# Pooling sums of an attention kernel: values summed in thirds on POOL, the keys' first level made over all partitions, with copies by ACT

## The chip, the cores and the metric
The kernel runs on one core of one Trainium2 chip. The metric is the time on the device in microseconds (us) of one execution, as the median of several runs.

## The reference
There are four batches of eight heads; each head has 576 tokens of 64 numbers, in float32. An attention with two branches feeds two mixture-of-experts layers with 8 experts each (width 512, hidden width 1024).

```python
q_d = q.reshape(B, H, Sd, 4, D).mean(axis=3)     # k_d, v_d alike: Sd = 144
out_up = np.repeat(sm_attn(q_d, k_d, v_d), 4, axis=2)
mask = np.abs(pos[:, None] - pos[None, :]) < 4   # the local branch: 7 keys for each query
out_local = softmax(where(mask, scale * q @ k.T, -1e9)) @ v
x = (out_up + out_local)  ->  [2304, 512]
x = moe(x, w1, w2, gates)                        # top 1 of 8: relu(x @ w1[e]) @ w2[e], weighted
x = moe2(x, w1, w2, gate)
```

The change concerns only how q, k and v are summed over groups of four tokens for the pooled branch (the division by four is folded into later scales).

## The kernel before
**Layout.** Two heads are stacked on the 128 partitions, so that partitions 0 to 63 hold one head of a pair and 64 to 127 the other; NP = 4 pairs make the eight heads. `kd` and `qt` hold keys and queries of a batch transposed (three buffers each, for batches b % 3). `vraw` holds the values of one batch in the order of the pooled branch, as 128 x (3 chunks of keys, 4 tokens of a group, 4 pairs, 65); it has one buffer, so the load of the next batch's values waits until the last sum of this one has read it.

**The sums of four.** `sums_q` and `sums_k` sum four neighbouring tokens. On DVE a single `tensor_reduce` does it (line 465). On POOL it takes two additions: a first level into a temporary `tm` (line 467), which halves four to two, and a second level (line 468). The keys' sums go into `kpd`, which is block diagonal: the upper 64 partitions are summed into one block and the lower 64 into the other, so `sums_k` runs its whole work once for each half of the partitions. `sums_v` (line 470) adds within `vraw` in place over 128 x 1560 elements (line 471), and then writes the second level of each half of the partitions, 64 x 780 elements, into the block-diagonal `vpd` (line 474).

**Who does what.** Batch 0 stands in a prologue (the string `PRO`): the keys' sums and `sums_v` are on DVE (steps F0, F2 and V0), two pairs at a time. The queries of pairs 0 and 1 need no sums there (the product with them is made four times instead); those of pairs 2 and 3 are summed on DVE. In batch 1 the keys and values are summed by POOL and the queries by DVE; in batches 2 and 3 POOL sums all three.

**The loop behind it.** A software pipeline takes one tile of up to 116 tokens of the local branch in each step: scores on PE, `smax` on DVE (lines 614 and 618, both read PSUM), exponentials on ACT (L623), `norm` on DVE (lines 627 to 630, from SBUF to SBUF), transposes on PE (L635) that ACT evacuates, and the products with the values (L663). The pooled branch of the next batch is mixed in: scores (L503, L512), `smax` (L521, L524), exponentials (L531), transposes (L538), the product with `vpd` (L552, L558), and its `norm` (lines 574 to 584; L584 subtracts one SBUF tensor from another). After each group of four or five tiles `route` finds the expert and the place of every token (lines 254 to 360), in many short DVE instructions; `place` (lines 307 to 338) and `spread` (lines 340 to 353, `am` and `oc` from DVE, `bm` from ACT) feed PE's `list` products (L357). One PSUM bank (`misc`) serves in turn the gate's logits (L377) and the counts `pos` (read by L309 and L311).

**Order.** The scheduler of the language plans the order on each engine by a timeline of its own, from the program's order; the engines then run their queues in order. The experts follow the attention, with PE as the engine that is nearly always busy.

Of the kernel before, what the change touches and what calls it, by code (L numbers as in the profile page):

```python
# [9 lines left out]
F32 = mybir.dt.float32  # L10
# [4 lines left out]
ALU = mybir.AluOpType  # L15
# [5 lines left out]
B, H, S, D = 4, 8, 576, 64  # L21
NP = H // 2
SD = S // 4
# [157 lines left out]
def moe_pair_kernel(  # L181
# [17 lines left out]
    nc = tc.nc  # L199
# [189 lines left out]
    def attention(actx, early, early_x, front):  # L389
# [3 lines left out]
        sb2 = actx.enter_context(tc.tile_pool(name="a_sb2", bufs=2, side="right"))  # L393
# [5 lines left out]
        kd, qt = kq  # L399
        vd = [side[i].tile([128, NG, NP, D], F32, name=f"vd{i}") for i in range(2)]  # L400
        kpd = [side[i].tile([128, 2, NP, SD], F32, name=f"kpd{i}") for i in range(2)]
        vraw = sbe.tile([128, 3, 4, NP, 65], F32, name="vraw")
        vpd = [side[i].tile([128, 3, 2, NP, 65], F32, name=f"vpd{i}") for i in range(2)]
# [38 lines left out]
        def sums_k(b, c, n, eng=None):  # L442
            eng = eng or nc.vector
            a = slice(c, c + n)
            tm = tmp() if eng is nc.gpsimd else None
            for s in range(2):
                o = slice(64 * s, 64 * s + 64)
                src = kd[b % 3][o, a, 3:3 + S].rearrange("p a (t r) -> p a t r", r=4)
                pool4(eng, kpd[b % 2][o, s, a], src, tm[o, 0:n] if tm else None)

        def sums_q(b, c, n, eng=None):
            eng = eng or nc.vector
# [7 lines left out]
        def tmp():  # L460
            return sbe.tile([128, 2, SD, 2], F32, tag="tm", name="tm", bufs=2)

        def pool4(eng, dst, src, tm):
            if tm is None:
                eng.tensor_reduce(dst, src, axis=AX.X, op=ALU.add)
                return
            eng.tensor_tensor(tm, src[:, :, :, 0:2], src[:, :, :, 2:4], op=ALU.add)
            eng.tensor_tensor(dst, tm[:, :, :, 0], tm[:, :, :, 1], op=ALU.add)

        def sums_v(b, eng=nc.gpsimd):  # L470
            eng.tensor_tensor(vraw[:, :, 0:2], vraw[:, :, 0:2], vraw[:, :, 2:4], op=ALU.add)
            for s in range(2):
                o = 64 * s
                eng.tensor_tensor(
                    vpd[b % 2][o:o + 64, :, s], vraw[o:o + 64, :, 0], vraw[o:o + 64, :, 1], op=ALU.add
                )

        def sums(b, eng_q=None):
            for c in (0, 2):
                sums_k(b, c, 2, nc.gpsimd)  # L480
                sums_q(b, c, 2, eng_q or nc.gpsimd)
# [264 lines left out]
        for i in range(3):  # L746
            t = sb3.tile([128, 3, 128], F32, tag="p", name="p")
# [19 lines left out]
        def first(c):  # L767
            sums_k(0, c, 2, nc.gpsimd if c and KPOOL else None)
            if QPE < c + 2:
                sums_q(0, c, 2)  # L770
# [5 lines left out]
        def sums1(c):  # L776
            sums_k(1, c, 2, None if S1[c] == "d" else nc.gpsimd)
            sums_q(1, c, 2, None if S1[c + 1] == "d" else nc.gpsimd)

        pro = {  # L780
            "F0": lambda: first(0),
            "F2": lambda: first(2),
            "V0": lambda: sums_v(0, nc.vector),
            "Ls": lambda: (loc[0].scores(), loc[0].smax()),
            "Le": loc[0].exps,
# [7 lines left out]
            "lqk": lambda: load_qk(1),  # L793
            "lw1": lambda: (load_vw(1), load_qk(2)),
            "V1": lambda: sums_v(1),
            "A0": lambda: sums1(0),
            "A2": lambda: sums1(2),
# [8 lines left out]
        for s in range(-1, NL + 3):  # L806
# [6 lines left out]
            if 0 <= s:  # L813
                b, r = s // NTP + 1, s % NTP
                if b + 1 < B:
                    if r == 0:
                        load_vr(b + 1)
                    if r == (1 if s > 4 else 2):
                        sums_v(b + 1)
                    if r == 0 and b == 2:  # L820
                        load_qk(3)
                if 2 <= b < B and r == 0:
                    sums(b)
# [86 lines left out]
            if 6 <= s < 12:  # L910
                o = 384 * (s - 6)
# [704 lines left out]
```

## Time and profile before
| | |
|---|---|
| time, median of 3 runs | 759.45 us (757.87 to 759.95) |
| the profiled execution | 755.45 us |
| its span | 753.7 us |
| mean granted TensorE clock, share of full speed | 0.967 |
| busy share of the span: PE, DVE, ACT, POOL | 93%, 61%, 45%, 23% |

PE is TensorE's matmuls, DVE is VectorE, ACT is ScalarE, POOL is GpSimd. In a row of the timeline stand the start and the duration in us, the engine, the line, the operation, the tile written and the tiles read with their shapes, how many instructions are merged in the row (x2), and in brackets the engine's idle time before it and what ended it. In a row of a tile's view stand the least, median and greatest duration in ns and the first and last start in us. In a row of the windows stand the window, its length, and for each engine its busy time in it; then the granted TensorE clock, the share of time of the DMA engines and GB/s.

### The profile page before, as it was taken

To read this page: it belongs to the slowest core of one execution; us is meant where nothing else is said; L and a number is where in the kernel's file an instruction comes from. 1 tells how busy PE (TensorE), PEld (TensorE's weight loads), DVE (VectorE), ACT (ScalarE), POOL (GpSimd) and SP (SyncE) were. 2 spreads that over 40 slices of the span, in tenths; PEclk is the share of its full clock that TensorE was granted. 3 is DMA by queue.
4 is the path that set the end of the run, shared out by engine and by line. 5 is a ranking of instruction groups with operands and counts; after the bars stand their busy time and mean duration, and the time that the engine had idled before them with its cause. 6 is when DMAs were issued, how large, how long until landed. Compare 5 with 4: busy or idle time off the path is not lost. (4 is left out here: it accounts for less than half of the span.)

```text
span 753.7 us, 15825 instructions
## 1 busy us (share of the span) xinstructions
PE 700.1 (93%) x6048; PEld 642.4 (85%) x6048; DVE 460.0 (61%) x1169; ACT 342.4 (45%) x630; POOL 173.5 (23%) x202
## 2 busy tenths in 40 slices
PE   6788699995989999999999999989999999999993
PEld 4557477874979999999999999978999999999992
DVE  8787968786847656565757777535434444455520
ACT  2244366574444435345454463235425353554530
POOL 5774800001031203031211120152013030311111
PEclk9899989996999999999999999989999999999997
DMA  9935635135167535364555452256443544655500
GB/s 359 407 117 205 213 116 186 49 119 169 34 217 220 166 120 171 128 201 134 164 193 167 165 179 97 93 187 214 137 137 130 158 159 155 196 173 192 161 21 16
DMA packets 52990, 120.99 MB, mean 161 GB/s; under 512 B 4800, under 2 KB 26176, under 8 KB 51884
## 3 DMA queue, kind: packets, MB, share of 16 engines
q1 hardware_dynamic: 45772, 99.19, 39.6%
q0 software_dynamic: 7136, 20.72, 8.0%
q8 instruction: 50, 0.82, 0.4%
q14 instruction: 32, 0.26, 0.1%
HBM read 101.01 MB, written 20.71 MB: 162 GB/s over the span
## 5 line engine op out<-in xcount | busy, mean ns | idle before, releaser
L1123 DVE TENSOR_TENSOR wl<-raw,wh 128x1024 fp32r<-128x1024 f32 x128 | 156.2, 1224 | 111.2 <-ACT wh L1115 111.1
L1115 ACT CAST wh<-raw 128x1024 fp32r<-128x1024 f32 x128 | 133.1, 1048 | 199.1 <-PE py L1277 114.3
L1277 PE MATMUL ph<-xl,wh 128*128 128x256 f32 (+8 forms) x576 | 178.1, 311 | 0.2 <-DVE xl L1201 0.2
L1276 PE MATMUL ph<-xh,wh 128*128 128x256 f32 (+8 forms) x576 | 175.0, 312 | 2.6 <-DVE xl L1201 1.9
L1278 PE MATMUL ph<-xh,wl 128*128 128x256 f32 (+8 forms) x576 | 177.2, 309 | 0.0
L1276 PE MATMUL py<-h,wh 128*128 128x256 f32 (+8 forms) x448 | 138.5, 316 | 0.0
L1277 PE MATMUL py<-h,wh 128*128 128x256 f32 (+8 forms) x448 | 137.8, 311 | 0.0
L1278 PE MATMUL py<-h,wl 128*128 128x256 f32 (+8 forms) x448 | 137.3, 309 | 0.0
L1276 PEld LDWEIGHTS ph<-xh,wh 128*128 128x128 f32 x576 | 110.6, 195 | 4.8 <-DVE xl L1201 2.0
L1277 PEld LDWEIGHTS ph<-xl,wh 128*128 128x128 f32 x576 | 111.5, 194 | 1.1 <-DVE xl L1201 0.5
L1278 PEld LDWEIGHTS ph<-xh,wl 128*128 128x128 f32 x576 | 111.5, 194 | 0.6
L1403 DVE SCALAR_TENSOR_TENSOR h<-ph,h 128x256 fp32r<-128x256 f32 (+8 forms) x144 | 66.3, 471 | 40.9 <-ACT h L1402 40.4
L1402 ACT ACTIVATE h<-ph 128x256 fp32r<-128x256 f32 (+8 forms) x144 | 60.8, 423 | 55.9 <-PE ph L1278 54.7
L1277 PEld LDWEIGHTS py<-h,wh 128*128 128x128 f32 x448 | 84.2, 188 | 0.6
L1278 PEld LDWEIGHTS py<-h,wl 128*128 128x128 f32 x448 | 84.1, 188 | 0.6
L1276 PEld LDWEIGHTS py<-h,wh 128*128 128x128 f32 x448 | 83.5, 188 | 0.8
L1144 POOL DMA_INDIRECT xr<-x,ri x49 | 49.9, 1019 | 102.3 <-PE t L1194 79.4
L1204 POOL DMA_INDIRECT out<-yr,ri x25 | 25.8, 1031 | 128.9 <-ACT yr L1222 84.6
L1204 POOL DMA_INDIRECT x<-yr,ri x24 | 24.4, 1016 | 126.5 <-ACT yr L1222 118.0
L1476 DVE COPY yT<-py 128x256 f32<-128x256 f32 (+8 forms) x28 | 13.7, 489 | 39.9 <-PE py L1278 39.9
L1201 DVE TENSOR_TENSOR xl<-t,xh 128x512 fp32r<-128x512 f32 (+5 forms) x49 | 30.1, 620 | 12.2 <-ACT xh L1198 12.0
L1194 PE MATMUL t<-ident,xr 128*128 128x128 f32 (+5 forms) x196 | 29.6, 272 | 8.5 <-DMA xr<-x,ri 8.5
(193 smaller groups left out, 1037.3 us busy)
## 6 DMA issues: line engine op xcount, KB each, us to landing
raw<-w_a SPq DMA_DIRECT2D x64, 512.0 KB
raw<-w_b SPq DMA_DIRECT2D x64, 512.0 KB
vraw<-vr SPq DMA_DIRECT2D x4, 1560.0 KB
vd<-vw SPq DMA_DIRECT2D x4, 1280.0 KB
kd<-kT SPq DMA_DIRECT2D x8, 586.0 KB
qt<-qT SPq DMA_DIRECT2D x8, 586.0 KB
x<-zx SPq DMA_DIRECT2D x6, 768.0 KB
x<-x SPq DMA_DIRECT2D x36, 116.0 KB
```

What stands on the lines that cost most here:

```text
L1115: i = nc.scalar.copy(hi, raw)
L1123: i = nc.vector.tensor_tensor(lo, raw, hi.bitcast(F32), op=ALU.subtract)
L1144: g = nc.gpsimd.indirect_dma_start(xr[0:mm], None, src, bass.IndirectOffsetOnAxis(ap=ri[0:mm, k, 0:1], axis=0))
L1194: nc.tensor.transpose(pt[:, d, 0:mm], xr[0:mm, 128 * d:128 * d + 128], ident[0:mm, 0:mm])
L1201: nc.vector.tensor_tensor(xl[:, :, o], pt[:, :, 0:mm], xh[:, :, o].bitcast(F32), op=ALU.subtract)
L1204: i = nc.gpsimd.indirect_dma_start(M.dst[:, :], bass.IndirectOffsetOnAxis(ap=ri[0:mm, k, 1:2], axis=0), yr[0:mm], None, bounds_check=NT - ...
L1276: nc.tensor.matmul(ps, lhsT=ah, rhs=bh, start=first, stop=False)
L1277: nc.tensor.matmul(ps, lhsT=ah, rhs=bl, start=False, stop=False)
L1278: nc.tensor.matmul(ps, lhsT=al, rhs=bh, start=False, stop=last)
L1402: nc.scalar.activation(a[:, 0:n], ph[:, 0:n], func=AF.Relu)
L1403: nc.vector.scalar_tensor_tensor(b_[:, 0:n], ph[:, 0:n], 0.0, a[:, 0:n].bitcast(F32), op0=ALU.max, op1=ALU.subtract)
L1476: nc.vector.tensor_copy(yT[:, dc, 0:n], py[:, 0:n])
```

## The change
The keys' sums: on DVE (batch 0) one `tensor_reduce` over all 128 partitions writes a temporary `ks` with one buffer, and two copies by ACT put its halves in their blocks of `kpd`. On POOL (batches 1 to 3) the first addition is made once over all partitions, the second still for each half. The values' sums, on POOL and in batch 0 on DVE, go in three chunks: for each of the three, an addition of 128 x 520 and two of 64 x 260.

```diff
         def sums_k(b, c, n, eng=None):
             eng = eng or nc.vector
             a = slice(c, c + n)
-            tm = tmp() if eng is nc.gpsimd else None
+            src = kd[b % 3][:, a, 3:3 + S].rearrange("p a (t r) -> p a t r", r=4)
+            if eng is nc.vector:
+                tm = sb2.tile([128, 2, SD], F32, tag="ks", name="ks", bufs=1)[:, 0:n]
+                pool4(eng, tm, src, None)
+            else:
+                tm = tmp()[:, 0:n]
+                eng.tensor_tensor(tm, src[:, :, :, 0:2], src[:, :, :, 2:4], op=ALU.add)
             for s in range(2):
                 o = slice(64 * s, 64 * s + 64)
-                src = kd[b % 3][o, a, 3:3 + S].rearrange("p a (t r) -> p a t r", r=4)
-                pool4(eng, kpd[b % 2][o, s, a], src, tm[o, 0:n] if tm else None)
+                if eng is nc.vector:
+                    nc.scalar.copy(kpd[b % 2][o, s, a], tm[o])
+                else:
+                    eng.tensor_tensor(kpd[b % 2][o, s, a], tm[o, :, :, 0], tm[o, :, :, 1], op=ALU.add)
...
         def sums_v(b, eng=nc.gpsimd):
-            eng.tensor_tensor(vraw[:, :, 0:2], vraw[:, :, 0:2], vraw[:, :, 2:4], op=ALU.add)
-            for s in range(2):
-                o = 64 * s
-                eng.tensor_tensor(
-                    vpd[b % 2][o:o + 64, :, s], vraw[o:o + 64, :, 0], vraw[o:o + 64, :, 1], op=ALU.add
-                )
+            for k in range(3):
+                eng.tensor_tensor(vraw[:, k, 0:2], vraw[:, k, 0:2], vraw[:, k, 2:4], op=ALU.add)
+                for s in range(2):
+                    o = slice(64 * s, 64 * s + 64)
+                    eng.tensor_tensor(vpd[b % 2][o, k, s], vraw[o, k, 0], vraw[o, k, 1], op=ALU.add)
```

## Rows read from the trace of the kernel before
**Rows 1.** Windows: busy time of each engine in stretches of the span.
```profile
8.00:29.00 21.00, 13.08 (x117) 10.42 (x116) 20.65 (x37) 5.83 (x13) 10.08 (x11) 0.84 1.02 413
...
84.00:97.00 13.00, 6.37 (x104) 4.65 (x105) 12.96 (x33) 4.96 (x14) 7.17 (x3) 0.85 0.42 157
97.00:160.00 63.00, 61.43 (x1059) 49.75 (x1058) 49.19 (x180) 38.64 (x95) 0.00 (x0) 0.98 0.33 108
...
280.00:400.00 120.00, 120.00 (x872) 115.67 (x871) 76.33 (x210) 58.21 (x97) 26.30 (x35) 1.00 0.51 165
```
**Rows 2.** Timeline of DVE in the first batch, 4 to 22 us.
```profile
4.62 2.73 DVE L465 TENSOR_REDUCE kpd<-kd 64x288 f32<-64x1152 f32 x2 [1.78 <-DMA kd<-kT]
7.97 2.71 DVE L465 TENSOR_REDUCE kpd<-kd 64x288 f32<-64x1152 f32 x2 [0.62 <-DMA kd<-kT]
10.72 1.35 DVE L465 TENSOR_REDUCE qd<-qt 128x288 f32<-128x1152 f32 x1
...
14.04 1.77 DVE L471 TENSOR_TENSOR vraw<-vraw 128x1560 f32<-128x1560 f32 x1
...
17.66 2.83 DVE L474 TENSOR_TENSOR vpd<-vraw 64x780 f32<-64x780 f32 x2
20.52 0.82 DVE L524 TENSOR_TENSOR pd<-s,pmx 128x288 f32<-128x288 f32 x2
```
**Rows 3.** Timeline of PE, where it had stood idle ahead of 60 us.
```profile
21.08 2.41 PE L538 MATMUL t<-ident,pd 128*128 128x128 f32 x9 [5.77 <-issue]
...
47.22 0.55 PE L538 MATMUL t<-ident,pd 128*128 128x128 f32 x3 [2.49 <-ACT pd L531]
```
**Rows 4.** Timeline of ACT: its first work after the table load.
```profile
13.20 0.81 ACT L531 ACTIVATE pd<-pd 128x288 f32<-128x288 f32 x2 [11.18 <-DVE pd L524]
```
**Rows 5.** Tile vraw: the sums of the values on both engines.
```profile
L474 POOL TENSOR_TENSOR vpd<-vraw x6: 1817/1838/2283, 47.1 to 90.9; 64x780 f32<-64x780 f32 x6
...
L471 POOL TENSOR_TENSOR vraw<-vraw x3: 3484/3501/3511, 42.2 to 85.5; 128x1560 f32<-128x1560 f32 x3
L474 DVE TENSOR_TENSOR vpd<-vraw x2: 990/1400/1810, 17.7 to 18.7; 64x780 f32<-64x780 f32 x2
```
**Rows 6.** Tile tm: the first level of keys and queries on POOL.
```profile
L467 POOL TENSOR_TENSOR tm<-kd x12: 1136/1144/1764, 16.7 to 78.8; 64x576 f32<-64x576 f32 x12
L467 POOL TENSOR_TENSOR tm<-qt x4: 1197/1206/1206, 34.9 to 80.0; 128x576 f32<-128x576 f32 x4
```
**Rows 7.** Timeline of DVE, 27 to 46 us: additions from SBUF to SBUF.
```profile
27.73 0.69 DVE L630 TENSOR_TENSOR p<-p,sm 128x512 f32<-128x512 f32 x1
...
29.23 0.43 DVE L584 TENSOR_TENSOR odl<-od,odh 128x256 fp32r<-128x256 f32 x1 [0.47 <-ACT odh L583]
...
40.17 1.53 DVE L630 TENSOR_TENSOR p<-p,sm 128x512 f32<-128x512 f32 x1
41.63 4.20 DVE L584 TENSOR_TENSOR od2l<-od,od2h 128x128 fp32r<-128x128 f32 x1
```
**Rows 8.** Timeline of POOL in the same stretch.
```profile
41.11 1.11 POOL L468 TENSOR_TENSOR kpd<-tm 64x288 f32<-64x288 f32 x1
42.19 3.48 POOL L471 TENSOR_TENSOR vraw<-vraw 128x1560 f32<-128x1560 f32 x1
```
**Rows 9.** Timeline of DVE, 86 to 93 us: three short instructions of route's place.
```profile
86.09 2.88 DVE L327 SCALAR_TENSOR_TENSOR den<-den,ez 128x5 f32<-128x5 f32 x1
...
89.12 1.79 DVE L310 TENSOR_TENSOR pe<-pe,oh 128x40 f32<-128x40 f32 x1
...
91.10 1.69 DVE L336 COPY v<-gh 128x5 f32<-128x5 f32 x1
```
**Rows 10.** Timeline of PE in the same stretch, after its two longest idle times.
```profile
91.13 0.42 PE L377 MATMUL lT<-xT,wg 128*32 128x128 f32 x8 [2.74 <-DVE gh L334]
...
95.85 0.73 PE L357 MATMUL list<-bm,am 128*128 128x432 f32 x1 [3.56 <-ACT bm L348]
```

## The prediction, made before the changed kernel was built or run
> **What bounds the kernel now.** I read the busy time by stretches first, to see which engine sets the pace where. In the experts' part PE is busy all the time (120.00 of 120 us in the stretch shown), and from 97 to 160 us nearly so, 61.43 of 63 [rows 1]. Whatever is won ahead of 97 us should therefore reach the end one for one, since behind that point the same PE work waits for its turn. Ahead of it there are two stretches in which DVE and not PE is full: 8 to 29 us (DVE 20.65 of 21, PE 13.08) and 84 to 97 us (DVE 12.96 of 13, PE 6.37) [rows 1]. The change works in both, and in a place between.
>
> Then the timelines of DVE, and of POOL and PE beside it. Three places matter.
>
> First batch. DVE sums the keys in two pairs of reduces, at 4.62 and 7.97 us; each pair had waited for its keys to land. Behind the second it has work without a break, the queries' sum, V0 (its additions at 14.04 and 17.66), and the subtraction at 20.52 [rows 2]. PE's transposes start at 21.08 after 5.77 us of idleness, just behind that subtraction, which frees a PSUM buffer [rows 3].
>
> At 42 us. A DVE subtraction of 128x128 begins at 41.63 and lasts 4.20 us, where one twice that size took 0.43 earlier [rows 7]. In the same stretch POOL ends an addition at 42.22 and has its first level of values, 3.48 us long, from 42.19 to 45.67 [rows 8]. DVE is let go at 45.83, as POOL ends. So an operation of DVE with two inputs in SBUF is held while POOL adds. PE lacked work for 2.49 us, up to 47.22 [rows 3].
>
> At 86 us. The same happens three times in a row: L327, L310 and L336, on 5 to 40 elements a partition, take 2.88, 1.79 and 1.69 us [rows 9], where 128x256 took 0.43 [rows 7]; at least 5.1 us of the 6.36 are waiting. POOL's first level begins at 85.5 and lasts 3.5, the two second-level additions 1.84 each, the last from 90.9 [rows 5]; each of the three is let go as one of POOL's ends. PE idles 2.74 us up to 91.13 (the logits wait for the bank that the place step reads) and 3.56 us up to 95.85 (the first list product) [rows 10].
>
> **The change part by part.**
>
> *Keys of batch 0.* Four reduces of half the partitions become two over all. One of 128x288 costs 1.35 us, a pair of halves 2.71 to 2.73 [rows 2], so 1.36 go twice. The first saving is not on the path: DVE would wait longer for the second keys, which landed at 7.97. The second is, since DVE runs on without a break: **-1.35 us**. Were nothing limited by landings, both would count, -2.7; if DVE then waits for the second queries, which come behind the keys, the gain is 0. The four copies by ACT, of 64x288, are about 0.4 us each, from ACT's 0.81 for two of 128x288; ACT stood idle for 11.18 us up to 13.20 [rows 4], so they hide there. Without that cover they would cost PE 0.8 us a pair.
>
> *Values of batch 0 on DVE.* The first level of 1.77 us becomes three of 128x520, 0.69 each by the 128x512 of [rows 7]; two second-level additions of 0.99 unheld [rows 5] become six of 64x260, 0.43 each by the 128x256 of [rows 7]. That is 2.07 + 2.58 against 1.77 + 1.98: **+0.90 us**, on the path by the same argument. Lower bound 0, if back-to-back starts hide the fixed parts. The upper bound has to take in the holds: one of the two second-level additions was held already (1.81 against 0.99 [rows 5]).
>
> *Keys on POOL.* Six additions of 64x576 go, at 1.14 us, and the six left grow to 1.20, the price of 128 partitions [rows 6]: 6.5 us of POOL over three batches. Count **0** for it: nothing found above waits for the keys' sums, only for POOL's hold to end.
>
> *Values on POOL.* 3.50 us become three of about 1.2 (a 128x576 took 1.20 [rows 6]), and two of 1.84 [rows 5] six of about 0.63. Over a batch this is 7.4 us where 7.2 were, so POOL gains nothing. What changes is how long one hold lasts. At 42 us, the held subtraction would be free after the first third, at 43.4 and not at 45.7, 2.3 us sooner. The later thirds will catch other DVE work, so I take **-2.0 us**; bounds 0 (POOL starts its next piece without a gap, as at 42.19) and -2.49, all that PE idled there.
>
> The Trainium skill, "SBUF — State Buffer", section "Who interferes with whom", says that a Vector instruction with two SBUF inputs and a GpSimd instruction that reads SBUF exclude each other for a whole instruction, and that whoever issues first wins. By it, the subtraction issued at 41.63 should have gone ahead of the addition issued at 42.19; the row shows it behind. By the rule the thirds give the full 2.3 us, by that row 0 where pieces follow without a gap.
>
> Around 86 us the same POOL work has to pass, and DVE is full, so the length of a hold matters less than how much DVE does between holds. Before, three instructions were caught in 7.2 us. With nine pieces DVE gets six more chances to slip one short instruction through, each with the unheld work around it, some 0.25 us (estimate from the unheld 0.43 of a far larger one): **-1.5 us**. Bounds: 0, if every chance is lost to the next piece, and -4.7, if L327 is let go 2.3 us sooner and the other two 1.2 each with nothing caught later. In batch 2 I count 0 either way, since I found no idle time of PE behind its sums.
>
> **Sum.** -1.35 + 0.90 - 2.0 - 1.5 = -3.95, say -4.0 us. The profiled execution took 755.45 us, so 751.45; the median of the runs, 759.45, stands 4.0 above it, and the forecast on that scale is 755.5. A measurement of this kernel can tell some 0.3%, 2.3 us, from no change.
>
> **The rivals.**
>
> *Thirds, but no handover (chance 0.22).* POOL's second piece starts as the first ends, and DVE stays locked out over all nine. For it: at 42.19 POOL went on although DVE had waited since 41.63 [rows 7, 8]. Against it: L327 ended at 88.97, with the first level, and L310 at 90.91, between the two second-level additions [rows 9], so DVE did get in twice; a second level also has to wait for the first. Then only the first batch counts, -0.45, and the place at 86 us perhaps -0.5: 758.5, no change that can be measured.
>
> *The gaps close altogether (0.17).* The clock granted to PE was 0.85 of full in 84 to 97 us, between its two levels of 1.2 and 2.4 GHz, after idle times of 2.74 and 3.56 us; it was 0.98 in the stretch behind [rows 1, 10]. If DVE's hold no longer makes these gaps, the products behind them also run at full clock: 2.49 at 42 us, 4.7 at 86, some 1.5 of clock (0.13 of 13 us is 1.7) and 0.45 in the first batch, -9: 750.5. Against it: DVE is full in that stretch even with 5.1 us of holds taken off (12.96 of 13, so 7.9 are work) and POOL's 7.2 us have to pass in it.
>
> *More pieces catch more DVE work (0.16), the slower side.* Each of the 27 pieces on POOL, and each of V0's nine on DVE, can hold the other engine. Before, POOL's values held DVE for 3.9 us at 42 and at least 5.1 at 86. DVE meets pieces all the time where it is full; at 86 us each of POOL's three caught one [rows 9]. If 16 or more of the 27 pieces catch an instruction on the path, at the mean of 7.4/9 = 0.8 us, they hold 13 us, against 9 now, and V0's pieces, held by POOL's 1.14 to 1.76 us additions that start at 16.7 [rows 6], add up to 1.8 more on two of them. From 14 pieces on it loses; 17 pieces give +4.6, with -0.45 and the 0.5 to 1 of a hold in V0 some +5: 764. Against it: POOL's values take 7.4 us instead of 7.2, so the time in which a hold can fall is the same, and an instruction that is caught waits for a third of what it waited for.
>
> **How the numbers follow.** My forecast, a gain of 2.3 to 6.5 us, has 0.45 and its own range is 753.0 to 757.2. The rivals have 0.22 (758.5), 0.17 (750.5) and 0.16 (764). Faster is the forecast with the second rival, less a little for forecasts that fall short of 2.3: 0.60. Same is the first rival and that little, 0.25. Slower is the third, 0.15. The range of 8 in 10 goes from the second rival's 750.5 to half way to the third's price: 750.0 to 761.0. The scheduler plans anew and may order other work differently; that is why the range doesn't stop at the first rival.
>
> **What would show it.** Right: two reduces of 128x288 from the keys, and four ACT copies ended ahead of 13 us; PE's first transposes ahead of 21.08; no DVE instruction at the first POOL values held for more than 1.3 us, and PE's 2.49 us idle time gone; in the last batch, DVE holds of 0.6 to 1.2 us each, more of them, and the list product ahead of 95.85 by more than the earlier gains. Wrong: DVE held across several pieces; or V0's nine additions spread past 21 us; or PE's gaps at 90 to 96 us as long as before; or a wait of equal length elsewhere, for the experts' first weights above all, that takes back what was won.

## The result and the profile after

| | before | after |
|---|---|---|
| median of the runs (4 each) | 758.89 us | 745.51 us (744.15 to 747.58) |
| ratio, with its 95% interval | | 0.9833 [0.9806, 0.9859] |
| the profiled execution | 755.45 us | 745.73 us |
| its span | 753.7 us | 744.0 us |

The kernel became 13.4 us faster by the medians and 9.7 by the two profiled executions; that of before lies 3.4 us under its median, that of after 0.2 above. The forecast was 755.5 us with a range from 750.0 to 761.0: the direction was right, and the time lies below the range.

The first view is that of the windows of the changed kernel: window, length, busy time of PE, PEld, DVE, ACT and POOL, then the granted clock.

```profile
8.00:29.00 21.00, 13.25 (x113) 10.19 (x112) 20.18 (x38) 6.55 (x14) 6.88 (x9) 0.82 1.02 414
29.00:38.00 9.00, 8.04 (x42) 4.71 (x43) 3.77 (x13) 1.29 (x3) 1.86 (x3) 0.67 0.93 382
...
84.00:97.00 13.00, 11.08 (x147) 8.42 (x145) 12.35 (x35) 9.77 (x28) 6.57 (x6) 1.00 0.70 249
97.00:160.00 63.00, 59.85 (x1083) 49.03 (x1082) 50.06 (x189) 38.89 (x96) 2.72 (x5) 1.00 0.39 139
```

The stretch from 84 to 97 us has changed most. PE works 11.08 us of 13, where it worked 6.37, at a granted clock of 1.00 where it was 0.85 [rows 1]. DVE is as full as before, but with the work of a later tile; PE is nearly full from 97 us on, as it was. The first batch has gained nothing: DVE is still full in it (20.18 us of 21), and behind it, from 29 to 38 us, the granted clock is 0.67, between PE's two levels of 1.2 and 2.4 GHz (more on that below).

To see where the time comes from, I followed the same matmuls on PE through both traces. The order of the instructions differs somewhat between 12 and 15 us and from 54 us on (below), but the same 1108 matmuls stand ahead of the first product with `od2h` of batch 1's last tile.

| what PE begins | before | after | difference | forecast of the step |
|---|---|---|---|---|
| first product with `odh` | 34.03 | 36.97 | +2.9 | -0.45 |
| batch 1's first transposes of `pd` | 47.22 | 47.51 | +0.3 (step -2.65) | -2.0 |
| first product with `od2h`, batch 1's last tile | 107.19 | 96.19 | -11.0 (step -11.3) | -1.5 |
| first transposes of the experts | 177.02 | 167.25 | -9.8 | 0 |
| end of the span | 753.7 | 744.0 | -9.7 | 0 |

Behind the experts' first transposes nothing more is won or lost, as predicted; 1.2 us are lost between the last tile and them. The gain lies between 47 and 107 us.

**First batch.** The timeline of DVE and that of PE in the changed kernel:

```profile
4.49 1.35 DVE L473 TENSOR_REDUCE ks<-kd 128x288 f32<-128x1152 f32 x1 [1.65 <-DMA kd<-kT]
7.78 1.35 DVE L473 TENSOR_REDUCE ks<-kd 128x288 f32<-128x1152 f32 x1 [1.94 <-DMA kd<-kT]
...
14.18 1.91 DVE L480 TENSOR_TENSOR vraw<-vraw 128x520 f32<-128x520 f32 x3
...
16.97 1.75 DVE L483 TENSOR_TENSOR vpd<-vraw 64x260 f32<-64x260 f32 x2
...
19.48 3.36 DVE L483 TENSOR_TENSOR vpd<-vraw 64x260 f32<-64x260 f32 x4
```
```profile
21.64 0.80 PE L559 MATMUL v<-vpd,pts 128*128 128x130 f32 x2 [2.31 <-DVE vpd L483]
...
29.34 0.73 PE L247 MATMUL list<-zb,za 128*128 128x432 f32 x1 [3.04 <-DVE za L246]
```

The keys cost what was predicted, 1.35 us for a pair instead of 2.71 and 2.73 [rows 2]. The six second-level additions of V0 take 5.11 us instead of the 2.58 worked out: POOL's sums for batch 1 hold them. PE waits for their pieces (2.31 us), and then 3.04 us for `za`, the zeros that open the list product.

The 2.9 us by which the first product with `odh` is later have two parts. The product with `za` begins at 29.34 us instead of 27.64, and that is the work of V0's pieces: in the five traces with V0 in nine pieces it begins at 28.68 to 30.46, in all others at 26.74 to 28.19. The other 1.2 us came with the granted clock behind it, and this can't be put down to the change. The windows of the kernel before, and of an experiment below ("whole values behind the places") whose program and order on PE are those of the kernel before up to there:

```profile
29.00:38.00 9.00, 8.24 (x106) 5.55 (x110) 3.94 (x10) 3.01 (x7) 6.05 (x7) 1.00 0.93 383
```
```profile
29.00:38.00 9.00, 8.38 (x43) 4.48 (x42) 2.65 (x7) 1.17 (x4) 3.40 (x4) 0.64 0.93 383
```

With the same program the first product with `odh` came, in these two, at 34.03 us at a clock of 1.00 and at 36.68 at 0.64. So two traces of the same program can differ by some 2.7 us from here on. The trace of the kernel before is an early one; that may be a part of the 3.4 us by which it lies under its median.

**At 42 us.** One view with DVE and POOL together:

```profile
43.06 1.53 POOL L475 TENSOR_TENSOR tm<-qt 128x576 f32<-128x576 f32 x1
43.46 1.29 DVE L591 TENSOR_TENSOR od2l<-od,od2h 128x128 fp32r<-128x128 f32 x1
44.56 3.83 POOL L480 TENSOR_TENSOR vraw<-vraw 128x520 f32<-128x520 f32 x3
```

The subtraction takes 1.29 us instead of 4.20 [rows 7], and PE's idle time of 2.49 us is gone [rows 3]. But the thirds are not what let it in: it came while POOL added queries (L475) and was done at 44.75, about as the first third began. Before, one half of the keys' second level stood ahead of the values [rows 8].

**At 86 us.** The short instructions of `place`, in DVE's timeline, and POOL's values in its own:

```profile
81.50 0.57 DVE L310 TENSOR_TENSOR pe<-pe,oh 128x40 f32<-128x40 f32 x1
...
83.09 0.15 DVE L327 SCALAR_TENSOR_TENSOR den<-den,ez 128x5 f32<-128x5 f32 x1
...
85.15 0.16 DVE L336 COPY v<-gh 128x5 f32<-128x5 f32 x1
```
```profile
76.71 5.29 POOL L483 TENSOR_TENSOR vpd<-vraw 64x260 f32<-64x260 f32 x6
...
90.28 4.23 POOL L480 TENSOR_TENSOR vraw<-vraw 128x520 f32<-128x520 f32 x3 [7.53 <-DMA vraw<-vr]
94.47 5.26 POOL L483 TENSOR_TENSOR vpd<-vraw 64x260 f32<-64x260 f32 x6
```

L327, L310 and L336 took 2.88, 1.79 and 1.69 us [rows 9]; now they take 0.15, 0.57 and 0.16. They don't slip between the pieces of batch 3's values: they meet none of them (L310 meets the last piece of batch 2's, which ends at 82.00). These instructions run 3 to 8 us earlier, and batch 3's values come 4.8 us later (85.5 before [rows 5]), because their one buffer is loaded again only when batch 2's second level has read it, at 82.00. Behind `place` the thirds do meet DVE, and there each holds one instruction and lets it in at its end: L637, `am` and `odl` take 1.35, 1.30 and 1.52 us, where their like beside them took 0.65, 0.28 and 0.42.

```profile
90.78 1.35 DVE L637 TENSOR_TENSOR p<-p,sm 128x512 f32<-128x512 f32 x1
92.05 1.30 DVE L344 TENSOR_SCALAR am<-cs,pp 128x128 fp32r<-128x128 f32 x1
93.27 1.52 DVE L591 TENSOR_TENSOR odl<-od,odh 128x256 fp32r<-128x256 f32 x1
```

What is left on PE there is one idle time, for this `am`, in its timeline:

```profile
93.49 0.43 PE L357 MATMUL list<-bm,am 128*128 128x432 f32 x1 [1.88 <-DVE am L344]
```

### The profile page after: what moved, and what is told of

It reads as the page before. It is cut to its first block, busy times and chain, and to the rows that moved or that the text cites. A ratio compares the mean times of both kernels' runs of the same rounds, so it can differ in the third digit from the quotient of the medians.

```text
span 744.0 us, 15847 instructions
## 1 busy us (share of the span) xinstructions
PE 700.1 (94%) x6048; PEld 640.2 (86%) x6048; DVE 450.5 (61%) x1173; ACT 343.5 (46%) x634; POOL 173.2 (23%) x214
## 5 line engine op out<-in xcount | busy, mean ns | idle before, releaser
L1151 POOL DMA_INDIRECT xr<-x,ri x49 | 52.1, 1063 | 98.1 <-PE t L1201 77.2
L1205 ACT CAST xh<-t 128x512 fp32r<-128x512 f32 (+5 forms) x49 | 26.1, 532 | 24.4 <-PE t L1201 21.2
```

Of the source, the lines that this page charges most:

```text
L1151: g = nc.gpsimd.indirect_dma_start(xr[0:mm], None, src, bass.IndirectOffsetOnAxis(ap=ri[0:mm, k, 0:1], axis=0))
L1205: i = nc.scalar.copy(xh[:, :, o], pt[:, :, 0:mm])
```

## The experiments

Each was timed beside runs of the kernel before on the same chip (medians 757.7 to 758.7 us). The expectations speak of "the od2h product of batch 1" and "of batch 2"; by the code these belong to the last tiles of batches 0 and 1. A stretch between them compares well only between kernels with the same order on PE: ahead of the first of the two stand 495 to 507 matmuls in most kernels, but 558 in the changed one.

### The change in its parts

```diff
 # thirds_only: sums_v as in the change, sums_k as before
 # keys_only: sums_k as in the change, sums_v as before
 # v0_whole: the change, but on DVE (batch 0)
+            if eng is nc.vector:  # the three additions of before
 # thirds_pool_only: the kernel before, but on POOL
+            for k in range(3):    # the nine additions of the change
 # keys_pool_only, keys_dve_only: the new sums_k on the one engine alone
```

Thirds on both engines: 

> The values in thirds on both engines, the keys' sums as in the kernel before. Theory H (the gain is that POOL's values hold DVE for less long at once): nearly the whole gain, 10 to 13 us faster than before, with the first batch late as in the changed kernel (V0 in nine pieces). Theory K (the gain is POOL being through with the keys sooner, and the plan that follows from it): 0 to 3 us faster, and the place at 86 us as slow as before.

Keys on both engines: 

> The keys' first level over all partitions with ACT's copies, the values whole as before. Theory H: within 2 us of the kernel before, a DVE subtraction held for about 4 us at POOL's first values again, and PE's transposes in the first batch 1 to 3 us sooner. Theory K: 8 us faster or more.

The change with V0 whole: 

> The changed kernel, but the first batch's values (on DVE) in three additions instead of nine. If V0's nine pieces made the first batch late (PE's product with the first pooled result at 36.97 us instead of 34.03): 2 to 4 us faster than the changed kernel, PE's clock not lowered at 29 to 38 us, and that product ahead of 34. If the lateness comes from the new plan for the keys: as the changed kernel.

Thirds on POOL alone: 

> The kernel before with POOL's values alone in thirds; the keys and the first batch's values as before. Theory H: the first batch as before, and all of the later gain of the changed kernel, so 12 to 16 us faster than before. Theory K: 0 to 3 us faster.

Keys on POOL alone: 

> Of the keys' edit only the part on POOL (one first level over all partitions), the first batch's keys and all values as before. If the keys' gain of 4.9 us comes from POOL (other order, other meeting places with DVE): 4 to 5 us faster than before. If it comes from the first batch (DVE's reduces and ACT's copies): 0 to 1 us.

Keys on DVE and ACT alone: 

> The kernel before with the keys' sums of batch 0 alone as in the change (two reduces over all partitions, four copies by ACT); POOL as before. By the prediction's term: 756.4, 1.35 us less. By the two runs that bound it (both engines 752.94, POOL alone 748.87) it wins nothing: 757 to 760, and the subtraction at 42 us is held 3 to 4 us as in the kernel before.

| kernel | median, us | ratio to before | the subtraction at 42 us took, us |
|---|---|---|---|
| thirds on both engines | 751.27 | 0.9922 [0.9891, 0.9953] | 4.48 |
| thirds on POOL alone | 754.88 | 0.9972 [0.9946, 0.9997] | 4.48 |
| keys on both engines | 752.94 | 0.9935 [0.9909, 0.9960] | 1.29 |
| keys on POOL alone | 748.87 | 0.9886 [0.9838, 0.9934] | 1.29 |
| keys on DVE and ACT alone | 758.61 | 1.0004 [0.9986, 1.0022] | 4.20 |
| the change, V0 whole | 745.70 | 0.9839 [0.9806, 0.9872] | 1.29 |

In the first batch nothing is worth anything at the end: V0 whole gives the changed kernel's time, and the keys' edit on DVE gives that of before, where 1.35 us less was predicted. The keys' edit on POOL, which I had counted 0, wins 8.9 us by itself, and 5.0 together with its part on DVE (their runs overlap: 746.53 to 752.98 and 749.69 to 753.43). The thirds by themselves win 3 us on POOL (6.6 on both engines, with runs from 748.91 to 758.07), and 7.2 us on top of the keys' edit (752.94 to 745.70; PE's order is the same in these two). Neither theory of the first expectations came true as a whole: H asked for 10 to 16 us from the thirds, K for 8 us or more from the keys on both engines. In the thirds alone, the subtraction is held across all three, as one view of DVE and POOL shows for thirds on POOL alone:

```profile
42.68 1.11 POOL L468 TENSOR_TENSOR kpd<-tm 64x288 f32<-64x288 f32 x1
43.19 4.48 DVE L591 TENSOR_TENSOR od2l<-od,od2h 128x128 fp32r<-128x128 f32 x1
43.76 3.77 POOL L480 TENSOR_TENSOR vraw<-vraw 128x520 f32<-128x520 f32 x3
47.60 0.66 POOL L468 TENSOR_TENSOR kpd<-tm 64x288 f32<-64x288 f32 x1
```

With the keys on POOL alone the values are whole, and yet it is let in, at the end of the queries' addition:

```profile
39.25 1.54 POOL L486 TENSOR_TENSOR tm<-qt 128x576 f32<-128x576 f32 x1
39.65 1.29 DVE L603 TENSOR_TENSOR od2l<-od,od2h 128x128 fp32r<-128x128 f32 x1
40.75 3.55 POOL L490 TENSOR_TENSOR vraw<-vraw 128x1560 f32<-128x1560 f32 x1
```

### What stands in front of the values

Three kernels move one addition in POOL's order. In the first, whole values; in the third, thirds on POOL; both with the keys' sums as before. The second is the changed kernel with half of a keys' second level put ahead of its thirds.

```diff
 # swap, thirds_swap: one constraint of order; the second level of batch 2's
 # keys (pairs 2 and 3) stands behind the first level of batch 1's values
+                if (b, c) == (2, 2):
+                    behind(i)
 # half_ahead: only the second half does, and the queries' first level too
+                    if (b, c, s) == (2, 2, 1):
+                        behind(i)
```

Whole values behind the queries' addition: 

> The kernel before, with two additions on POOL in another order: the first level of batch 1's values follows the queries' addition over 128 partitions (line 467 of the kernel before) and no longer one half of the keys' second level over 64. In four traces the DVE subtraction at 42 us was held for 3.9 to 4.2 us where that half addition stood in front of the values, even in thirds, and for 1.0 us where the full one did, even with whole values. Theory F (what stands in front of the values decides): held for about 1 us, PE's idle time of 2.5 us gone, 2 to 3 us faster than before. Theory L (the length of the values' addition decides): held for about 4 us, within 1 us of the kernel before.

Half a keys' addition ahead of the thirds: 

> The changed kernel, with the half addition of the keys put in front of the thirds of batch 1's values, the other half and the queries' addition behind them. Theory F: the subtraction is held for about 4 us over all three thirds, PE idles for 2.5 us, 2 to 3 us slower than the changed kernel. Theory L: held for at most 1.3 us, as the changed kernel.

Thirds behind the queries' addition: 

> The kernel before with POOL's values in thirds (754.88 us by itself), and the first level of batch 1's values moved behind the queries' addition of 128x576 instead of behind one half of the keys' second level. Theory F (what stands in front of the values decides whether DVE is let in at the boundaries: behind a POOL addition on 64 partitions the held subtraction of od2l is passed by all three thirds, behind one on 128 partitions it gets in at the first boundary): the subtraction is held 1.0 to 1.3 us instead of 4.2, PE's idle time of 2.8 us at 49 us goes, and the median is 750 to 753. Rival L (only the length of a piece and where the subtraction falls in it): held up to 4 us again, and 754 to 757.

The first missed: 757.09 us, ratio 0.9992 [0.9969, 1.0015]. The subtraction came 0.5 us after the whole addition had begun and was held to its end. So the length of a piece counts as well.

```profile
42.62 3.94 POOL L482 TENSOR_TENSOR vraw<-vraw 128x1560 f32<-128x1560 f32 x1
43.13 3.58 DVE L597 TENSOR_TENSOR od2l<-od,od2h 128x128 fp32r<-128x128 f32 x1
```

The second lost 8.7 us against the changed kernel: 754.22 us, 0.9945 [0.9913, 0.9977]. (The scheduler also gave it another order on PE, 507 matmuls ahead of the first `od2h` product; the last experiments price that.) Its view of DVE and POOL has another short instruction, held over all three thirds behind the half addition:

```profile
41.30 0.66 POOL L466 TENSOR_TENSOR kpd<-tm 64x288 f32<-64x288 f32 x1
41.69 4.04 DVE L650 TENSOR_SCALAR sm<-sm 128x8 f32<-128x8 f32 x1
41.93 3.77 POOL L493 TENSOR_TENSOR vraw<-vraw 128x520 f32<-128x520 f32 x3
45.77 0.66 POOL L466 TENSOR_TENSOR kpd<-tm 64x288 f32<-64x288 f32 x1
```

The third came out as theory F said: 749.69 us, 0.9903 [0.9883, 0.9923], 5.2 us below the same thirds behind the half addition, with the same order on PE up to the experts. The subtraction met the first third itself and took 1.38 us:

```profile
42.86 1.21 POOL L478 TENSOR_TENSOR tm<-qt 128x576 f32<-128x576 f32 x1
...
44.02 4.28 POOL L491 TENSOR_TENSOR vraw<-vraw 128x520 f32<-128x520 f32 x3
44.54 1.38 DVE L604 TENSOR_TENSOR od2l<-od,od2h 128x128 fp32r<-128x128 f32 x1
```

### Where batch 3's values meet the place step

```diff
 # before_no_v3, after_no_v3, swap_no_v3: batch 3's values aren't summed
-                    if r == (1 if s > 4 else 2):
+                    if r == (1 if s > 4 else 2) and b + 1 < 3:
                         sums_v(b + 1)
 # v3_behind: they wait for the places of group 0;
 # half_v3_late, v3_late: for the last list product of group 0
+                if b == 3:
+                    tc.add_manual_dep(i.ins, last_put[0].ins.name, ...)
...
-                    if r == (1 if s > 4 else 2):
+                    if r == 2 and s < 5:
                         sums_v(b + 1)
+                if s == 13:
+                    sums_v(3)
                     if r == 0 and b == 2:
                         load_qk(3)
```

The last two issue these sums behind some of batch 3's products, which then use what `vpd` held before. They also leave out the load of batch 3's keys and queries: `load_qk(3)` now hangs below `s == 13`, where `r` is 3 and not 0. In their DMA views stand 6 transfers of `kd<-kT` and 6 of `qt<-qT`, in that of the changed kernel 8 of each. So what they won or lost can't be put down to the later sums.

Whole values behind the places: 

> The kernel before, with POOL's sums of the last batch's values made to wait until DVE has placed the tokens of the first group (key of line 321), so that they no longer meet lines 309 to 336. Theory P (the changed kernel gains at 84 to 97 us because its values come later, behind the place step): the stretch from the second to the third product with od2h, 47.2 us before and 35.1 changed, takes 39 to 42; 5 to 8 us faster than before. Theory H (only shorter holds help): the whole values hold DVE for 5 us elsewhere in a stretch where it is full; within 2 us of the kernel before.

The kernel before without these sums: 

> The kernel before without the sums of batch 3's values (the products of batch 3 then use what vpd holds, so its output there isn't the reference's): the price of those sums for the engines beside them. If the holds of the place step around 86 us carry most of what the change won, as their 5.1 us of waiting and PE's 2.74 and 3.56 us of idle time say, it takes 748 to 752, and the stretch of PE from the od2h product of batch 1 to that of batch 2 goes from 47.2 us to 38 to 41. If the stretch is long for another reason (DVE is full there by its own work), 755 to 758.

Half a keys' addition ahead, batch 3's values late: 

> The kernel with one half of a keys' addition put ahead of the thirds of batch 1 (754.22 us), with batch 3's values' sums moved behind the list products of group 0. Theory C (the time lost at 42 us makes batch 3's sums meet the place step of group 0, and that meeting costs most of it): the hold at 42 us stays near 3.9 us, the stretch of PE from the od2h product of batch 1 to that of batch 2 falls from 42.7 to 35 to 38 us, and the median is 747.5 to 750. Rival D (the loss adds up over many small holds in the first half): 752.5 to 755.

The changed kernel with V0 whole, batch 3's values late: 

> The changed kernel with batch 0's values in whole additions on DVE (745.7 us), and batch 3's values' sums moved behind the list products of group 0. By theory C the changed kernel has little left there (2.8 us of holds and 1.88 us of PE's idle time): 743.5 to 745.7. By rival D no change, 745 to 746.5. If the later sums hold up batch 3's product with the values instead: 747 to 750.

Thirds behind the queries' addition, without these sums: 

> The thirds behind the queries' addition (749.69 us by itself), without the sums of batch 3's values (its output in batch 3 isn't the reference's); the keys' sums are as before. If the two meetings are the whole of the gain, the median is 744 to 747, what the changed kernel takes. If POOL's shorter list of keys wins by itself, it stays at 747.5 to 749.5: taking the second meeting away then wins less than 2 us, because PE idled only 3.65 us ahead of the first list product here.

The changed kernel without these sums: 

> The changed kernel without the sums of batch 3's values (its output in batch 3 isn't the reference's). In the kernel before the same cut won 6.6 us. If the changed kernel has got past that meeting, 743.5 to 745.5, 0 to 2 us less than its own 745.5; if it still pays half of it, 741.5 to 743.

| kernel | median, us | ratio to before | against the same kernel with the sums in place, us |
|---|---|---|---|
| before, whole values behind the places | 758.07 | 1.0005 [0.9976, 1.0034] | 0 |
| before, without the sums | 751.15 | 0.9926 [0.9898, 0.9955] | -6.6 |
| half ahead, sums late, batch 3's keys and queries not loaded | 750.69 | 0.9915 [0.9896, 0.9933] | -3.5 |
| changed, V0 whole, sums late, batch 3's keys and queries not loaded | 744.78 | 0.9823 [0.9799, 0.9848] | -0.9 |
| thirds behind the queries, without the sums | 747.77 | 0.9854 [0.9811, 0.9897] | -1.9 |
| changed, without the sums | 749.66 | 0.9883 [0.9841, 0.9925] | +4.2 |

In the kernel before, these sums beside `place` cost 6.6 us; the first list product begins at 91.46 us without them and at 95.85 with them [rows 10]. Where the hold at 42 us has been shortened, with the thirds behind the queries' addition, taking them away gains 1.9; there the two meetings are not the whole of the gain, which asked for 744 to 747. The two kernels with late sums (0.9 and 3.5 us faster, the second 0.7 above theory C's range) decide nothing, since they lack a load as well, and the first has another order on PE; whether part of what the hold at 42 us costs is paid here isn't shown by them. The miss with whole values behind the places shows that to be late is not enough: at 92.37 they held the next instructions, a pair of L345 for 3.82 us.

The traces of all kernels show how the two places hang together. Where the hold at 42 us is short (1.29 to 1.38 us, nine traces), L310 of this `place` begins at 79.94 to 83.91 us; where it is long, or another instruction is held for 4.04 us there (ten traces), at 86.46 to 93.13. And where it is short, batch 3's values begin at 81.05 and 81.74 us if they are whole, in the two kernels with the keys' edit alone, and at 88.78 to 90.28 if they are in thirds and the rest is loaded and summed as it should be. Of the kernels that sum these values at their usual place, those with both, a short hold and thirds, are through with L321 of `place` when the values begin, and so is the one with thirds on both engines (95.31 against 98.10 us); in all others the two overlap.

The last row is a miss that I can follow only in part. Up to batch 1's last tile this kernel is ahead of the changed one (95.61 against 96.19, although its first product with `odh` began 0.93 later), which is the small gain expected. Behind it, with the same order on PE, PE idles 2.76 us for ACT's `x`, where it idled 0.95 in the changed kernel. In the timeline of PE and in the windows:

```profile
122.87 0.58 PE L654 MATMUL v<-odh,rep 128*128 128x256 f32 x1 [2.76 <-ACT x L679]
```
```profile
120.00:127.00 7.00, 4.24 (x17) 3.85 (x17) 3.69 (x12) 3.64 (x10) 0.00 (x0) 0.63 0.34 127
127.00:135.00 8.00, 7.76 (x117) 6.13 (x117) 5.36 (x15) 4.16 (x9) 0.00 (x0) 0.90 0.14 53
```

The granted clock is 0.63 there and 0.90 behind (in the changed kernel 1.00 in both windows), and the next batch's like product comes at 133.99 instead of 130.04. ACT's copy into `x` is late because it waits for its buffer: an earlier store of `x` hasn't landed. In ACT's timeline it waits 3.39 us for that, in the changed kernel 1.59:

```profile
122.23 0.59 ACT L679 COPY x<-v 128x512 f32<-128x512 f32 x1 [3.39 <-DMA x<-x]
```
```profile
121.00 0.58 ACT L679 COPY x<-v 128x512 f32<-128x512 f32 x1 [1.59 <-DMA x<-x]
```

Why the store lands later without these sums wasn't tried.

### The order on PE as a rival

With the keys' edit on POOL the scheduler also finishes batch 0's fourth tile ahead of the fifth one's first products. Two kernels have this order (558 matmuls ahead of the first `od2h` product) without the edit:

```diff
+                        if (b, t, s, i) == (0, NTP - 1, 0, 0):
+                            tc.add_manual_dep(m.ins, last_vd[0].ins.name, ...)  # order alone
```

The kernel before: 

> The kernel before with one constraint on PE's order: the first product of batch 0's fifth tile with the pooled values stands behind the last product of the fourth tile, as in the changed kernel. POOL's additions are as before. Rival O (the order that the scheduler chose with the keys' edit, and not POOL's work, is what the term counted 0 really gave): 749 to 753, as with the keys' edit alone, although the subtraction at 42 us is still held 3 to 4 us. Theory K (POOL's shorter list and what it puts in front of the values): 756 to 759.

Thirds behind the queries' addition: 

> POOL's values in thirds, behind the queries' addition (749.69 us by itself), and the same constraint on PE's order; the keys' sums as before. If hold, thirds and order are the whole of the gain: 744.5 to 747, the changed kernel's time without its edit of the keys. If POOL's shorter list of keys is needed besides: 748.5 to 750.5.

By itself the order wins nothing: 758.61 us, 1.0001 [0.9982, 1.0019], with the subtraction held 4.20 us as before. With the hold shortened it wins 3: 746.65 us, 0.9844 [0.9820, 0.9868], 1.1 above the changed kernel, without the edit of the keys. In the first of the two, PE's timeline shows the gap of 2.49 us again and a longer one at another place:

```profile
50.30 0.90 PE L538 MATMUL t<-ident,pd 128*128 128x128 f32 x3 [2.49 <-ACT pd L531]
...
100.30 2.94 PE L552 MATMUL v<-vpd,pts 128*128 128x130 f32 x12 [5.42 <-DVE pd L524]
```

No kernel that does the whole work was faster than the changed one by more than the measurement can tell.

## Why the prediction was wrong

**Right:** that what is won ahead of 97 us reaches the end nearly one for one (11.0 us at the last tile, 9.7 at the end); that the two holds of DVE by POOL's values, at 42 and at 86 us, are where the time lies; the price of a reduce over all partitions; that ACT's copies hide.

**The step that failed** is "Keys on POOL. Count **0** for it: nothing found above waits for the keys' sums, only for POOL's hold to end." The keys' sums decide when that hold begins and what DVE meets. With the edit on POOL alone, the subtraction at 42 us comes under a queries' addition and gets in at its end, and the kernel takes 748.87 us instead of 757.74. PE's changed order is no explanation by itself (758.61); with the hold shortened it adds 3.0 us (749.69 to 746.65). How the 8.9 us divide among the hold, the order and POOL's shorter list stays open.

**At 42 us** the size was right (-2.65 of PE's time, -2.0 predicted) and the cause wrong. "The held subtraction would be free after the first third" didn't happen in either kernel with the thirds alone: it took 4.48 us, across all three. That is the observation that the first rival, thirds but no handover, asked for, though over three pieces and not all nine. That the size fits is luck: the changed kernel has no hold by a third at this place. The handover comes with what stands in front of the values, and the thirds use it: behind the queries' addition they give 749.69 us, where whole values give 757.09.

**Around 86 us** the term of -1.5 us was the one mis-sized, and its mechanism was at most a part. I counted shorter catches of `place`; in the changed kernel batch 3's values no longer meet `place`. The shorter catches are there behind it, three of 0.7 to 1.1 us in `spread` and its neighbours. In the kernel before, the meeting cost 6.6 us, more than the 5.1 of holds that I read from [rows 9]. `place` is earlier where the hold at 42 us is short, and the values are later in thirds, because nine pieces end later and so start the load later. How much of the 11.3 us in this stretch belongs to each of the two, and how much to the shorter pieces that are met, stays open.

**In the first batch** I predicted -0.45 us; PE's product with `za` came 1.7 us later, for V0's pieces were held by POOL as the third rival said, and spread past 21 us, to 22.84, a sign of being wrong that I had named. The rest of the 2.9 us at `odh` goes with the granted clock. It cost the end nothing that can be measured: the changed kernel with V0 whole has the product with `za` at 26.90 and takes 745.70 us.

**The rivals.** The second, that the gaps close altogether, came true in the trace as to the time: -9 there, 9.7 measured, with PE's idle times of 2.49, 2.74 and 3.56 us behind 40 us replaced by one of 1.88, and the granted clock at 1.00 instead of 0.85. I held against it that DVE is full in that stretch; it is still (12.35 us of 13), with the next work. That the totals agree is partly luck: the rival had 6.2 us around 86 us with the clock and 0.45 in the first batch, where 11.3 were won and 2.9 lost. Of the 10.0 us between forecast and median, 5.7 are in the trace (751.45 against 745.73). The rest is the scale: I took a trace 4.0 us below the median as typical of both kernels, and that of the changed kernel lies at its median.

## What to carry to other kernels

Before a shared resource's work is counted at 0 because nobody waits for its result, look at what it pushes aside: here a shorter list on POOL moved a hold of 3.9 us off DVE's path, and that edit alone, with the order on PE that came with it, took 8.9 us off, more than all that was aimed at. Splitting a long operation helps only if the other engine is let in between the pieces, so look in the trace for a handover at just that boundary, with what runs ahead of it. And where two engines meet by timing, follow the same matmul through both traces and check that the order ahead of it is the same, before a stretch is compared. Look at the granted clock as well: the same program was 2.7 us apart in two traces for it.

## What the runs showed of the hardware

- **A waiting DVE instruction can be passed by several POOL additions.** If it came while POOL worked on 64 partitions (64x288) with the values next, it was passed by the whole first level: 4.19 or 4.20 us in the kernel before and four with its order of additions; 4.48, 4.48 and 4.04 us over three thirds. If it came under an addition over 128 partitions (128x576, 128x520), it was let in at its end: 1.29 us in five kernels, 1.38 with thirds behind the queries. It isn't a rule for all halves: L310 came under the first 64x780 addition and was let in at its end [rows 5, 9]. All eight of these long holds ended where POOL paused for the first time, for 0.07 or 0.08 us (in the rows with 4.48 and 4.04 shown, from 47.53 to 47.60 and from 45.70 to 45.77); the short ones ended without a pause. What tells the two apart wasn't tried. The Trainium skill, "SBUF — State Buffer", section "Who interferes with whom", has the engine that issues first win the port; that agrees with the 1.29 us rows and not with the 4.20 and 4.48.
- **Small instructions are held too, and such as read one tensor:** a TENSOR_SCALAR of 128x8 (4.04 us), a COPY of 128x5 (1.69 us [rows 9]) and, with the keys on POOL alone, a pair of 128x128 `am` (3.72 us for both). So the prediction's "two inputs in SBUF" was too narrow.
- **An idle time, then the lower clock:** in the changed kernel without batch 3's sums PE idles for 2.76 us up to 122.87. The granted clock is 1.00 from 120.10 to 121.70, while PE is already idle (0.01 us busy), and 0.50, its lower level of 1.2 GHz, from 122.90 to 128.50; so the idle time came first. The next batch's product came 4 us later. After 0.95 us of idle time at the same matmul of the changed kernel the row from 120 to 127 us shows 1.00.

```profile
120.10:121.70 1.60, 0.01 (x1) 0.00 (x0) 1.60 (x6) 0.00 (x0) 0.00 (x0) 1.00 0.92 342
122.90:128.50 5.60, 5.60 (x23) 4.98 (x23) 1.95 (x9) 2.98 (x9) 0.00 (x0) 0.50 0.13 50
```
